# Pooled attention and two feed-forward blocks: the attention scores as two 64-row products in place of one 128-row product with a block-diagonal operand

## The chip, the cores and the metric

The kernel runs on one core of a Trainium2 chip. The metric is the device time of one execution in microseconds (us). Three runs of the kernel before gave a median of 1476.97 us (1474.87 to 1482.33).

## The reference

Attention over keys and values that are averaged eight at a time, then two feed-forward blocks. Batch 8, 8 heads, 576 positions, head size 64, so 72 pooled keys per head:

```
k_p = k.reshape(B, H, Sp, pool, D).mean(axis=3)
v_p = v.reshape(B, H, Sp, pool, D).mean(axis=3)
scores = scale * np.matmul(q, k_p.transpose(0, 1, 3, 2))
scores = scores - np.max(scores, axis=-1, keepdims=True)
attn = np.exp(scores)
attn = attn / (np.sum(attn, axis=-1, keepdims=True) + 1e-09)
out = np.matmul(attn, v_p)
...
a = x @ w1
b = x @ w2
y = ((a * b) @ w3) @ w_out
...
h = y @ w_in
g = h * (1.0 / (1.0 + np.exp(-1.702 * h)))
result = g @ w_out2
```

`x` is the attention output as 4608 tokens of 512 features; w1 and w2 are 512 by 1024, w3 1024 by 1024, w_out 1024 by 512, w_in 512 by 2048, w_out2 2048 by 512.

## The kernel before, in words

Attention works in 32 groups of two heads (`NG`; group n is a batch and a pair of heads). The two heads of a group lie one above the other in the partitions: head 0 in rows 0 to 63, head 1 in rows 64 to 127. For a group,

- `g0` transposes the raw keys and queries on VectorE into `kT` and `qT` (128 rows by 576 positions; one buffer each), adds the keys up eight at a time into `ks` (128 by 72, line 258), and two ScalarE copies (lines 260 and 261) put the upper and the lower half of `ks` onto the diagonal of `kbd`, a 128 by 144 operand whose other two quarters were set to zero once (line 207);
- `g1` multiplies: for each of the five tiles of up to 128 positions (`tt`) one fp32 matmul (line 277) with the 128 by 128 tile of `qT` as the stationary operand and `kbd` as the moving one, so that 144 columns come out, 72 for each head. The first three tiles go to one PSUM bank, the other two to a second one; VectorE takes the maximum of each row and head (line 282) and subtracts it into `s_t` (line 284), bank by bank;
- `g2` is the exponential on ScalarE, `g3` the sum and the division and 32 by 32 transposes on VectorE, `g4` splits the weights into a high and a low part for the product in fp32r, `g6` multiplies by the pooled values (lines 380 to 383) and puts the result into `x`.

For the first four groups (`NPE`), `g4` transposes on TensorE (lines 351 to 361), and odd groups use the banks `acc2` and `acc3` in place of `wk2` and `wk3`.

The first feed-forward block runs in between. Every product of it is made of three fp32r matmuls of 512 columns (`mm3`, lines 114 to 116: high by high, high by low, low by high). `tick()` calls the next step of a group after each half of a feed-forward step, so that four ticks make a group once the first four are through. Weights arrive as 64-bit numbers, are turned into fp32 by `Conv.step` (ScalarE, VectorE, and GpSimd at line 172), and w3 is transposed on TensorE at line 508. A second part of the program (line 709 and on) holds the second feed-forward block and no attention.

The instructions are written by Python in this order, and the tile framework's scheduler sets the final order of each engine; the order within a call of `g1` is therefore not the order on the chip in every group.

An fp32 matmul stands in the trace as two records, each with its own load of the stationary operand (LDWEIGHTS, on the row PEld) and its own MATMUL; an fp32r matmul is one record.

Of the kernel before, what the change touches and what calls it, by code (L numbers as in the profile page):

```python
# [7 lines left out]
F32 = mybir.dt.float32  # L8
# [4 lines left out]
ALU = mybir.AluOpType  # L13
AX = mybir.AxisListType
# [3 lines left out]
P = 128  # L18
# [4 lines left out]
def pooled_attention_moe_moe2(  # L23
# [18 lines left out]
    nc = tc.nc  # L42
    B, H, S, D = q.shape
    NT, DM = out.shape
    POOL = 8
    SK = S // POOL
# [11 lines left out]
    TT = (S + P - 1) // P  # L58
    KW = 2 * SK
# [25 lines left out]
    def take(shape=(P, 2, T), dtype=F32R):  # L85
        pool, i = free.pop(0)
        t = pool.tile(list(shape), dtype, name=f"s{i}", tag=f"s{i}")
        held[id(t)] = (t, pool, i)
        return t

    def take_a(i, dtype=F32R):

        return slota_p.tile([P, 2, T], dtype, name=f"s{i}", tag=f"s{i}")
# [30 lines left out]
    def sl(i, n=P):  # L124
        return slice(i * n, (i + 1) * n)
# [65 lines left out]
    with pa_ctx:  # L191
        pa = pa_ctx.enter_context(tc.tile_pool(name="pa", bufs=1))
# [6 lines left out]
            out=mask[:, 0], in_=mask[:, 0], compare_op=ALU.is_gt, fill=0.0,  # L199
            base=SK, pattern=[[0, D]], channel_multiplier=-1)  # L200
        nc.gpsimd.affine_select(
            out=mask[:, 1], in_=mask[:, 1], compare_op=ALU.is_ge, fill=0.0,
            base=-SK, pattern=[[0, D]], channel_multiplier=1)
        qT = pa.tile([P, TT * P], F32, name="qT")
        nc.vector.memset(qT[:, S:], 0.0)
        kbd = pa.tile([P, 2, SK], F32, name="kbd")
        nc.vector.memset(kbd, 0.0)
        s_sl = take(dtype=F32)
        s_ts = [pa.tile([P, TT, PW], F32, name="s_t"), s_sl.rearrange("p a b -> p (a b)")[
            :, :TT * PW].rearrange("p (t w) -> p t w", w=PW)]  # L210
        for t in s_ts:
# [6 lines left out]
            out=ident, in_=ident, compare_op=ALU.is_equal, fill=0.0,  # L218
# [3 lines left out]
        nc.gpsimd.memset(f32(vt), 0.0)  # L222


        g_q, g_k, g_v, g_s = {}, {}, {}, {}

        def load_blocks(dst, src, b, hp):
            for c in range(4):
# [5 lines left out]
        def g_load(n):  # L234
            if n >= NG:
                return
            b, hp = divmod(n, HP)
            g_k[n] = pa.tile([P, S], F32, name="kr", tag="raw", bufs=4).rearrange("p (g d) -> p g d", d=32)
            load_blocks(g_k[n], k, b, hp)
            g_q[n] = pa.tile([P, S], F32, name="qr", tag="raw", bufs=4).rearrange("p (g d) -> p g d", d=32)  # L240
            load_blocks(g_q[n], q, b, hp)
# [10 lines left out]
        def g0(n):  # L252
            kr, qr = g_k.pop(n), g_q.pop(n)
            kT = pa.tile([P, S], F32, name="kT", tag="kT")
            nc.vector.transpose(out=kT, in_=kr.rearrange("p g d -> p (g d)"))
            nc.vector.transpose(out=qT[:, :S], in_=qr.rearrange("p g d -> p (g d)"))
            ks = pa.tile([P, SK], F32, name="ks", tag="ks")
            nc.vector.tensor_reduce(
                out=ks, in_=kT.rearrange("p (s u) -> p s u", u=POOL), op=ALU.add, axis=AX.X)
            nc.scalar.copy(kbd[:D, 0], ks[:D])  # L260
            nc.scalar.copy(kbd[D:, 1], ks[D:])
            g_load(n + 1)

        def banks_of(n):
            return acc[2:] if n < NPE and n % 2 else wk[2:]

        def s_of(n):
            return s_ts[n % 2 if n < NPE else 0]

        def g1(n):  # L270
            sc, s_t = banks_of(n), s_of(n)
            mov = kbd.rearrange("p a s -> p (a s)")
            nm = pa.tile([P, 2 * TT], F32, name="nm", tag="nm", bufs=2)
            for half, tts in ((0, range(0, 3)), (1, range(3, TT))):
                w = len(tts) * KW
                for i, tt in enumerate(tts):
                    nc.tensor.matmul(  # L277
                        sc[half][:, i * KW:(i + 1) * KW], qT[:, sl(tt)], mov,
                        start=True, stop=True)
                ps = sc[half][:, :w].rearrange("p (a s) -> p a s", s=SK)  # L280
                m = nm[:, 2 * tts[0]:2 * tts[-1] + 2]
                nc.vector.tensor_reduce(out=m, in_=ps, op=ALU.max, axis=AX.X)
                na = 2 * len(tts)
                nc.vector.tensor_tensor(
                    out=s_t[:, tts[0]:tts[-1] + 1, :KW].rearrange("p t (a s) -> p t a s", s=SK),
                    in0=ps.rearrange("p (t a) s -> p t a s", a=2),
                    in1=m.rearrange("p (t a) -> p t a", a=2).unsqueeze(3).to_broadcast(
                        [P, na // 2, 2, SK]),
                    op=ALU.subtract)

        def g2(n):
            s_t = s_of(n)
# [112 lines left out]
        def tick_first():  # L405

            t = tick_n[0]
            tick_n[0] += 1
            for n in range(NPE):
                if t == 2 * n + 6:  # L410
                    g6(n)
            for n in range(NPE):
                s = t - 2 * n
                if s == 0 and n == 0:
                    g0(0)
                elif s == 1:
                    g1(n)
                elif s == 2:
                    g2(n)
                    g0(n + 1)  # L420
                elif s == 3:
                    g3(n)
                elif s == 4:
                    g4(n)
                    g_va(n)
                elif s == 5:
                    g_vb(n)
            if t == 2 * NPE + 4:
                tick_n[0] = 4 * NPE
                give(s_sl)  # L430

        def tick():
            t = tick_n[0]
            if t < 4 * NPE:
                return tick_first()
            tick_n[0] += 1
            n, s = divmod(t, 4)
            if s == 0:
                if NPE <= n - 1 < NG:
                    g4(n - 1)  # L440
            elif s == 1:
                if n < NG:
                    g1(n)
            elif s == 2:
                if NPE <= n - 1 < NG:
                    g6(n - 1)
                if n < NG:
                    g2(n)
                    g_va(n)
                if n + 1 < NG:  # L450
                    g0(n + 1)
            elif n < NG:
                g3(n)
                g_vb(n)
# [147 lines left out]
        for blk in range(NB):  # L602
            x = [x_slot(blk, c) for c in range(KM)]
            if blk == NB - 2:

                pa_ctx.close()
                pa = pa_ctx.enter_context(tc.tile_pool(name="pc", bufs=1, reuse_waits="tile"))
# [10 lines left out]
            for f in range(NF1):  # L618
# [6 lines left out]
                if blk == NB - 1:  # L625
                    give(w1_s.pop(f))
                    give(w2_s.pop(f))
                    if 0 <= f - FA < KM:

                        t = take_a(f - FA)  # L630
# [6 lines left out]
                a = pa.tile([P, T], F32, name="a", tag="a", bufs=2)  # L637
# [34 lines left out]
    with tc.tile_pool(name="pb", bufs=1, reuse_waits="tile") as pb, \  # L672
# [206 lines left out]
        for k, f in enumerate(FO):  # L879
            bk = bank()  # L880
            w = ready.pop(("h", 0, f))
# [29 lines left out]
        for pr in range(1, NPAIR + 1):  # L911
# [17 lines left out]
            for fp in range(NFP):  # L929
# [4 lines left out]
                for name, i in ORDER:  # L934
# [6 lines left out]
                    if name in PART:  # L941
                        s, h = PART[name]
                        w = ready[s, pr, 2 * fp + i][:, h]
                    else:
                        w = ready[name, pr, fp][:, i]
# [66 lines left out]
            m1, U, V, n = [], [], [], 0  # L1012
# [116 lines left out]
```

## Time and profile before

| | |
|---|---|
| median of three runs | 1476.97 us (1474.87 to 1482.33) |
| the profiled execution | 1479.71 us, span 1478.0 us |
| TensorE matmul (PE) busy | 1438.7 us, 97% |
| stationary loads (PEld) busy | 1190.0 us, 81% |
| VectorE (DVE) busy | 988.7 us, 67% |
| ScalarE (ACT) busy | 693.9 us, 47% |
| GpSimd (POOL) busy | 489.0 us, 33% |

Busy shares are means over the whole span. A matmul's record is longer than the time that it adds to a stream, since matmuls overlap; what one adds is read from the distance between the starts of two. PEld lies beside PE. The score matmuls of the 32 groups lie between 24 and 601 us of the span.

### The profile page before, as it was taken

To read this page: it belongs to the slowest core of one execution; us is meant where nothing else is said; L and a number is where in the kernel's file an instruction comes from. 1 tells how busy PE (TensorE), PEld (TensorE's weight loads), DVE (VectorE), ACT (ScalarE), POOL (GpSimd) and SP (SyncE) were. 2 spreads that over 40 slices of the span, in tenths; PEclk is the share of its full clock that TensorE was granted. 3 is DMA by queue.
4 is the path that set the end of the run, shared out by engine and by line. 5 is a ranking of instruction groups with operands and counts; after the bars stand their busy time and mean duration, and the time that the engine had idled before them with its cause. 6 is when DMAs were issued, how large, how long until landed. Compare 5 with 4: busy or idle time off the path is not lost.

```text
span 1478.0 us, 19436 instructions
## 1 busy us (share of the span) xinstructions
PE 1438.7 (97%) x6536; PEld 1190.0 (81%) x6536; DVE 988.7 (67%) x1728; ACT 693.9 (47%) x1212; POOL 489.0 (33%) x589
## 2 busy tenths in 40 slices
PE   6979999999999999999999999999999999999998
PEld 4867888888888888888788887888788888888886
DVE  7888998878787877654737255683559354944554
ACT  7875444434343433366635344552455244534442
POOL 8789656554545555366733100000000000000000
PEclk9989999999999999999999999999999999999999
DMA  9992233323232311199879978877677766785665
GB/s 265 248 233 48 57 85 57 80 46 78 49 77 49 77 33 37 42 325 344 309 236 398 325 243 276 294 211 221 194 244 224 221 197 221 239 234 180 194 213 139
DMA packets 294436, 267.64 MB, mean 181 GB/s; under 512 B 201664, under 2 KB 226240, under 8 KB 294336
## 3 DMA queue, kind: packets, MB, share of 16 engines
q1 hardware_dynamic: 291648, 265.09, 59.8%
q10 hardware_dynamic: 2688, 1.31, 0.3%
q8 instruction: 52, 0.85, 0.2%
q14 instruction: 48, 0.39, 0.1%
HBM read 209.72 MB, written 56.62 MB: 180 GB/s over the span
## 4 chain that ended last, share of the span: by engine, by line
PE 82%; DMA 7%; DVE 5%; ACT 2%; SPq 2%; issue 1%; POOL 1%; DVEq 0%; ACTq 0%; POOLq 0%
PE bk L709 39%; PE wk L114 8%; PE wk L115 8%; PE wk L116 8%; PE acc L114 4%; PE acc L115 4%; PE acc L116 4%; PE wk L277 2%; DMA wud<-wt 2%; DVE p L314 1%; SPq L229 1%; DMA st<-wind 1%; PE bk L115 1%; PE bk L116 1%; PE bk L114 1%
## 5 line engine op out<-in xcount | busy, mean ns | idle before, releaser
L709 PE MATMUL bk<-mv,st 128*128 128x512 f32 x1152 | 272.6, 391 | 0.7 <-DMA st<-wud 0.7
L709 PE MATMUL bk<-xM,st 128*128 128x512 f32 x1092 | 259.0, 390 | 3.9 <-DMA st<-wind 3.7
L709 PEld LDWEIGHTS bk<-mv,st 128*128 128x128 f32 x1152 | 217.3, 189 | 46.3 <-issue 1.1
L709 PEld LDWEIGHTS bk<-xM,st 128*128 128x128 f32 x1092 | 204.5, 188 | 48.6 <-issue 2.5
L114 PE MATMUL wk<-s,s 128*128 128x512 f32 x576 | 227.0, 396 | 2.8 <-DVE a L641 1.2
L116 PE MATMUL wk<-s,s 128*128 128x512 f32 x576 | 224.9, 391 | 2.1 <-DVE s L105 2.1
L115 PE MATMUL wk<-s,s 128*128 128x512 f32 x576 | 224.9, 391 | 0.0
L314 DVE STREAM_TRANSPOSE p<-s_t 32x160 f32<-32x160 f32 (+1 forms) x560 | 178.5, 319 | 10.3
L114 PE MATMUL acc<-s,s 128*128 128x512 f32 x352 | 134.8, 406 | 8.2 <-ACT s L104 3.2
L115 PE MATMUL acc<-s,s 128*128 128x512 f32 x352 | 141.4, 402 | 0.9 <-POOL s L105 0.8
L116 PE MATMUL acc<-s,s 128*128 128x512 f32 x352 | 140.4, 399 | 0.0
L114 PEld LDWEIGHTS wk<-s,s 128*128 128x128 f32 x576 | 108.5, 189 | 26.2 <-DVE a L641 2.1
L116 PEld LDWEIGHTS wk<-s,s 128*128 128x128 f32 x576 | 108.3, 188 | 24.8 <-DVE s L105 2.3
L115 PEld LDWEIGHTS wk<-s,s 128*128 128x128 f32 x576 | 108.4, 188 | 22.1 <-DVE s L391 0.4
L105 DVE TENSOR_TENSOR mv<-g,mv 128x1024 fp32r<-128x1024 f32 x80 | 97.8, 1222 | 33.6 <-ACT mv L104 32.2
L104 ACT CAST mv<-g 128x1024 fp32r<-128x1024 f32 x80 | 84.3, 1054 | 71.8 <-PE bk L709 71.4
L172 POOL TENSOR_TENSOR cv<-cv,s 128x512 int32<-128x512 int32 x72 | 97.5, 1364 | 28.6 <-DVE cv L169 21.1
L105 POOL TENSOR_TENSOR s<-a,s 128x512 fp32r<-128x512 f32 x56 | 72.5, 1294 | 82.5 <-ACT s L104 62.7
L638 ACT COPY a<-wk 128x512 f32<-128x512 f32 x72 | 42.1, 585 | 110.5 <-PE wk L116 89.7
L369 POOL TENSOR_TENSOR ph<-p,ph 128x576 fp32r<-128x576 f32 x32 | 45.7, 1429 | 126.5 <-ACT ph L368 123.9
L114 PEld LDWEIGHTS acc<-s,s 128*128 128x128 f32 x352 | 67.8, 193 | 23.4 <-ACT s L104 5.2
L115 PEld LDWEIGHTS acc<-s,s 128*128 128x128 f32 x352 | 68.2, 194 | 15.0 <-POOL s L105 2.0
(190 smaller groups left out, 2357.9 us busy)
## 6 DMA issues: line engine op xcount, KB each, us to landing
st<-wud SPq DMA_DIRECT2D x96, 512.0 KB, 4.4
st<-wind SPq DMA_DIRECT2D x66, 512.0 KB, 4.7
st<-wind SPq DMA_DIRECT2D x76, 256.0 KB, 3.9
s<-in_moe_w_dram SPq DMA_DIRECT2D x32, 512.0 KB, 6.4
wind<-s SPq DMA_DIRECT2D x32, 512.0 KB, 5.4
s<-in_moe_w_out_dram SPq DMA_DIRECT2D x24, 512.0 KB, 6.5
kr<-in_k_dram SPq DMA_DIRECT2D x128, 72.0 KB, 2.6
qr<-in_q_dram SPq DMA_DIRECT2D x128, 72.0 KB, 2.6
```

The costliest lines, as they stand in the source:

```text
L104: nc.scalar.copy(dst[:, 0], src)
L105: lo_eng.tensor_tensor(out=dst[:, 1], in0=src, in1=f32(dst[:, 0]), op=ALU.subtract)
L114: nc.tensor.matmul(o, a[:, 0, a_sl], b[:, 0, b_sl], start=first, stop=False)
L115: nc.tensor.matmul(o, a[:, 0, a_sl], b[:, 1, b_sl], start=False, stop=False)
L116: nc.tensor.matmul(o, a[:, 1, a_sl], b[:, 0, b_sl], start=False, stop=last)
L172: nc.gpsimd.tensor_tensor(out=w.bitcast(I32), in0=w.bitcast(I32), in1=lo_w.bitcast(I32), op=ALU.add)
L229: nc.sync.dma_start(dst[32 * c:32 * c + 32], src[b, 2 * hp + c // 2, :, 32 * (c % 2):32 * (c % 2) + 32].rearrange("(g t) d -> t g d", t=32))
L277: nc.tensor.matmul(sc[half][:, i * KW:(i + 1) * KW], qT[:, sl(tt)], mov, start=True, stop=True)
L314: nc.vector.transpose(out=dst[:, :nt, 32 * c:32 * c + 32], in_=s_t[32 * c:32 * c + 32, :nt, 32 * r:32 * r + 32])
L369: nc.gpsimd.tensor_tensor(out=ph[:, 1], in0=s0, in1=f32(ph[:, 0]), op=ALU.subtract)
L638: nc.scalar.copy(a, pa_)
L709: nc.tensor.matmul(o, w[:, x, m], b[:, y], start=first and n == 0, stop=last and n == 2, skip_group_check=True)
```

## The change

Each head has a product of its own. For every tile of positions there are two fp32 matmuls, one on rows 0 to 63 and one on rows 64 to 127 of the array (`tile_position` (0, 0) and (64, 0)): the stationary operand is 64 rows by 128 columns of `qT`, the moving one 64 rows by 72 columns of `ks`. Head 0 goes to the first bank, head 1 to the second, five tiles of 72 columns in each. Maximum and subtraction go by head instead of by half of the tiles. `kbd`, its memset and its two copies are gone; `ks` itself is read by TensorE.

```diff
-        kbd = pa.tile([P, 2, SK], F32, name="kbd")
-        nc.vector.memset(kbd, 0.0)
...
-            nc.scalar.copy(kbd[:D, 0], ks[:D])
-            nc.scalar.copy(kbd[D:, 1], ks[D:])
+            g_ks[n] = ks
...
         def g1(n):
-            sc, s_t = banks_of(n), s_of(n)
-            mov = kbd.rearrange("p a s -> p (a s)")
-            nm = pa.tile([P, 2 * TT], F32, name="nm", tag="nm", bufs=2)
-            for half, tts in ((0, range(0, 3)), (1, range(3, TT))):
-                w = len(tts) * KW
-                for i, tt in enumerate(tts):
+            sc, s_t, ks = banks_of(n), s_of(n), g_ks.pop(n)
+            nm = pa.tile([P, 2, TT], F32, name="nm", tag="nm", bufs=2)
+            for tt in range(TT):
+                for h in range(2):
+                    hd = slice(h * D, (h + 1) * D)
                     nc.tensor.matmul(
-                        sc[half][:, i * KW:(i + 1) * KW], qT[:, sl(tt)], mov,
-                        start=True, stop=True)
-                ps = sc[half][:, :w].rearrange("p (a s) -> p a s", s=SK)
-                m = nm[:, 2 * tts[0]:2 * tts[-1] + 2]
-                nc.vector.tensor_reduce(out=m, in_=ps, op=ALU.max, axis=AX.X)
-                na = 2 * len(tts)
+                        sc[h][:, tt * SK:(tt + 1) * SK], qT[hd, sl(tt)], ks[hd],
+                        start=True, stop=True, tile_position=(h * D, 0))
+            for h in range(2):
+                ps = sc[h][:, :TT * SK].rearrange("p (t s) -> p t s", s=SK)
+                nc.vector.tensor_reduce(out=nm[:, h], in_=ps, op=ALU.max, axis=AX.X)
                 nc.vector.tensor_tensor(
-                    out=s_t[:, tts[0]:tts[-1] + 1, :KW].rearrange("p t (a s) -> p t a s", s=SK),
-                    in0=ps.rearrange("p (t a) s -> p t a s", a=2),
-                    in1=m.rearrange("p (t a) -> p t a", a=2).unsqueeze(3).to_broadcast(
-                        [P, na // 2, 2, SK]),
-                    op=ALU.subtract)
+                    out=s_t[:, :, h * SK:(h + 1) * SK], in0=ps,
+                    in1=nm[:, h].unsqueeze(2).to_broadcast([P, TT, SK]), op=ALU.subtract)
```

The built order of TensorE around one burst of scores in the later groups, before (line 277; `wk_72` and `wk_73` are the two score banks, `wk_70` and the `acc` tiles belong to the feed-forward block):

```order
L115 MATMUL acc_69<-s_3472,s_690 128x512
L116 MATMUL acc_69<-s_3472,s_690 128x512
L277 MATMUL wk_72<-kbd,qT 128x144 x3
L277 MATMUL wk_73<-kbd,qT 128x144 x2
L114 MATMUL wk_70<-s_2083,s_1375 128x512
```

and the same place now (line 273 is the score matmul of the changed kernel):

```order
L115 MATMUL acc_69<-s_3336,s_1129 128x512
L116 MATMUL acc_69<-s_3336,s_1129 128x512
L273 MATMUL wk_72<-ks,qT 128x72
L273 MATMUL wk_73<-ks,qT 128x72
L273 MATMUL wk_72<-ks,qT 128x72
L273 MATMUL wk_73<-ks,qT 128x72
```

The five matmuls have become ten, which change between the two heads; six more rows like the last two follow before the next line 114. The last 20 groups and the first four have this order.

The same engine in one of the groups between these (groups 4 to 11), before:

```order
L114 MATMUL acc_67<-s_1406,s_808 128x512
L277 MATMUL wk_73<-kbd,qT 128x144 x2
L115 MATMUL acc_67<-s_1406,s_808 128x512
L116 MATMUL acc_67<-s_1406,s_808 128x512
L277 MATMUL wk_72<-kbd,qT 128x144 x3
L114 MATMUL acc_68<-s_1406,s_808 128x512
```

and now:

```order
L116 MATMUL wk_70<-s_711,s_1471 128x512
L273 MATMUL wk_73<-ks,qT 128x72 x3
L273 MATMUL wk_72<-ks,qT 128x72 x4
L273 MATMUL wk_73<-ks,qT 128x72
L273 MATMUL wk_72<-ks,qT 128x72
L273 MATMUL wk_73<-ks,qT 128x72
L114 MATMUL wk_70<-s_823,s_1471 128x512
```

Here the scheduler has put several matmuls of one head behind one another; in all there are 36 unbroken bursts now, where there were 41.

## Rows read from the trace of the kernel before

**Rows 1.** TensorE by windows: window, length, PE busy (records), granted clock, DMA share, GB/s.

```profile
0.00:100.00 100.00, 78.79 (x361) 0.93 0.97 250
100.00:200.00 100.00, 94.83 (x445) 0.98 0.40 84
200.00:610.00 410.00, 410.00 (x1981) 1.00 0.26 56
```

**Rows 2.** Chain of waits in order of time, 430 to 460 us: start, length, what.

```profile
431.70 1.23 PE wk L277 x10
...
450.37 1.23 PE wk L277 x10
```

**Rows 3.** Groups by line on TensorE, 200 to 610 us: line, shapes, count, busy, mean.

```profile
L277 PE MATMUL wk<-kbd,qT 128*128 128x144 f32 x220 | 31.0, 285 | 0.0
```

**Rows 4.** Timeline of PE near 308 us: start, length, engine, line, operation, tiles, shapes.

```profile
308.19 0.29 PE L380 MATMUL wk<-ph,vm 128*128 128x288 f32 x1
308.32 0.30 PE L381 MATMUL wk<-ph,vm 128*128 128x288 f32 x1
```

**Rows 5.** Timeline of PEld, 23.9 to 24.06 us.

```profile
23.96 0.19 PEld L277 LDWEIGHTS wk<-kbd,qT 128*128 128x128 f32 x1 [1.18 <-ACT kbd L261]
```

**Rows 6.** Timeline of PEld, 24.15 to 24.18 us: the second load of that burst.

```profile
24.07 0.19 PEld L277 LDWEIGHTS wk<-kbd,qT 128*128 128x128 f32 x1
```

**Rows 7.** Timeline of PE, 60.9 to 62.6 us.

```profile
61.71 0.27 PE L508 MATMUL wk<-ident,cv 128*128 128x128 f32 x1
61.82 0.27 PE L360 MATMUL acc<-ident,s 128*32 128x128 f32 x1
62.02 0.23 PE L361 MATMUL acc<-ident,s 64*32 64x64 f32 x1
```

**Rows 8.** Timeline of PE, 38.0 to 39.3 us.

```profile
38.48 0.23 PE L361 MATMUL wk<-ident,s_t 64*32 64x64 f32 x1
38.64 0.50 PE L115 MATMUL acc<-s,s 128*128 128x512 f32 x1
38.98 0.40 PE L116 MATMUL acc<-s,s 128*128 128x512 f32 x1
39.22 0.39 PE L115 MATMUL acc<-s,s 128*128 128x512 f32 x1
```

**Rows 9.** Timeline of PEld, 62.1 to 62.22 us: loads of 32 and of 128 columns.

```profile
62.02 0.09 PEld L361 LDWEIGHTS acc<-ident,s 64*32 64x32 f32 x1 [0.21 <-issue]
62.18 0.14 PEld L508 LDWEIGHTS wk<-ident,cv 128*128 128x128 f32 x1
```

**Rows 10.** Timeline of PEld, 62.325 to 62.34 us: the load after that.

```profile
62.24 0.14 PEld L508 LDWEIGHTS wk<-ident,cv 128*128 128x128 f32 x1
```

**Rows 11.** Timeline of PEld, 56.9 to 57.9 us: a load of 64 rows.

```profile
57.36 0.14 PEld L354 LDWEIGHTS acc<-ident,s 64*128 64x128 f32 x1 [0.17 <-issue]
```

**Rows 12.** Groups by line and shape, whole run: shapes, count, busy, mean, idle before.

```profile
L277 PEld LDWEIGHTS wk<-kbd,qT 128*128 128x128 f32 x300 | 42.2, 191 | 4.5 <-ACT kbd L261 1.2 <-DVE s L391 0.2
...
L282 DVE TENSOR_REDUCE nm<-wk 128x6 f32<-128x432 f32 x30 | 17.8, 595 | 1.3 <-PE wk L277 1.3
...
L284 DVE TENSOR_TENSOR s_t<-wk,nm 128x432 f32<-128x432 f32 x30 | 17.3, 578 | 0.0
...
L284 DVE TENSOR_TENSOR s_t<-wk,nm 128x288 f32<-128x288 f32 x30 | 13.2, 440 | 0.0
L282 DVE TENSOR_REDUCE nm<-wk 128x4 f32<-128x288 f32 x30 | 13.2, 440 | 0.0
...
L260 ACT COPY kbd<-ks 64x72 f32<-64x72 f32 x32 | 8.0, 249 | 3.7 <-DVE ks L258 3.5
L261 ACT COPY kbd<-ks 64x72 f32<-64x72 f32 x32 | 8.0, 249 | 0.7
```

More of the change, by code (lines that the diff above doesn't have):

```diff
@@ L222, in pooled_attention_moe_moe2 @@
         nc.gpsimd.memset(f32(vt), 0.0)
-        g_q, g_k, g_v, g_s = {}, {}, {}, {}
+        g_q, g_k, g_v, g_s, g_ks = {}, {}, {}, {}, {}
         def load_blocks(dst, src, b, hp):
```

## The prediction

> **What bounds the kernel.** I read the busy time by windows first. From 200 to 610 us TensorE is busy without a gap, at the full granted clock, 2.4 GHz; before that it is not: it has 21.2 us of idle time in the first 100 us and 5.2 us in the next 100 [rows 1]. So there are two stretches with different rules. In the later one whatever TensorE gains or loses is gained or lost by the kernel; in the earlier one part of it falls into waits for ScalarE, VectorE and GpSimd.
>
> Then the chain of waits: every 18.67 us (450.37 less 431.70) it goes for 1.23 us through the ten records of the score matmuls of one group [rows 2]. So a score burst costs 1.23 us, of a record 0.123 us, and 32 bursts cost 39.4 us. 220 of the records lie from 200 us on [rows 3]: 22 groups in the full stretch, ten before it. After 601 us there are no scores, and the second block keeps its code.
>
> Then single records, to see what makes up 0.123 us. A record has to load its stationary operand and to stream its moving columns. A matmul of 288 columns is followed by the next after 0.13 us [rows 4]; a score record with 144 columns takes 0.123 us, so an fp32 record streams each column about twice. With 72 columns that is 0.06 us, estimated by proportion. The load: at the start of the first burst, where nothing streams, the second load begins 0.11 us after the first [rows 5, 6]. Today the load of the next record (0.11) hides behind the stream of this one (0.12). Both are nearly equal; **halving the stream leaves the load bare**.
>
> **The change part by part.**
>
> *Records.* Five fp32 matmuls become ten, so ten records become twenty, each with a load of 128 columns and a stream of 72. What a load of 64 rows costs in fp32 no row shows. From below: the loads of the fp32 transposes (another kind of matmul) take 0.06 us where one is bare, 62.24 less 62.18 [rows 9, 10]. From above: 0.11 [rows 5, 6]. Whether half of the rows makes a load shorter can be read from the lengths of such transposes' loads: 0.14 us with 128 rows and 128 columns [rows 9], 0.14 with 64 rows and 128 columns [rows 11], 0.09 with 64 rows and 32 columns [rows 9]. Length goes with columns, and the columns stay 128. So I take 0.11, the row of the same operation. If loads follow one another, a burst has 20 x 0.11 = 2.20 us of loads, and the last stream of 0.06 behind them.
>
> The Trainium skill, "TensorE: Matmul & The Clock Gate", section on LDWEIGHTS, speaks against this change in the same way: the time of a load goes by its columns, and 32 rows take as long as 128. By its formula (128 columns at 1.2 GHz) I estimate 107 ns, and the twenty loads would be 2.13 us in place of 2.20; the trace agrees as far as its rows reach.
>
> *Changing the shape of the array.* The changed bursts go from 128 rows to 64 and back. The program has four places with a 64-row matmul. Between two 128-row transposes 0.11 us pass (61.71 to 61.82), before a 64-row one 0.20 (to 62.02) [rows 7]: 0.09 more on the way in. On the way out, the 64-row matmul (64 columns, 0.05 us at the rate of the 0.11 for 128) is followed after 0.16 us [rows 8]: another 0.11. And the next matmul cannot hide its load: 0.34 to the one behind it instead of 0.24 [rows 8], 0.10 to 0.11. Together 0.31 us a burst. From below, nothing, if what these rows show belongs to the change of the column width there (32 columns) and not of the rows; I take 0.31, since entering L360 with 32 columns shows no such step (0.11).
>
> *Sum of a burst:* 2.20 + 0.06 + 0.31 = 2.57 us, 1.34 more than 1.23. In the full stretch: 22 x 1.34 = +29.5 us. Of the ten groups before 200 us I count half, between all and nothing, since TensorE partly waits there anyway: 10 x 1.34 / 2 = +6.7 us.
>
> *What goes away.* Two copies of 0.249 us a group on ScalarE [rows 12]. From 200 us on, TensorE never waits for it, so they are worth nothing there. In the first groups they stand between the sum of the keys and the first load: the whole run has 1.2 us of waits of the loads for line 261 [rows 12]. I take -0.7 us; the bounds are 0 and -2. The memset of `kbd` is one early VectorE instruction: nothing.
>
> *VectorE.* Two maxima and two subtractions a group before and after: (595 + 440) and (578 + 440) ns for 6 + 4 head-tiles [rows 12] become twice five, the same sum by proportion. Both banks are now complete only at the end of the burst, instead of the first one after three fifths of it; the one wait known there is 1.3 us in the whole run [rows 12]. Nothing, while TensorE has other work; at most another 1 us early. `ks` has one buffer and is now read by the matmuls, so the sum of the next group (line 258) waits for them; `qT`, also with one buffer, is refilled on the same engine after the same matmuls already, so no new wait arises. GpSimd's instructions and the DMA issues stay the same in number; where the scheduler sets them otherwise in the first groups, I count nothing. The four bursts more than groups (36 against 32) would cost 4 x 0.31 = 1.2 us, inside the half that is open there.
>
> *Sum:* 29.5 + 6.7 - 0.7 = +35.5 us on the profiled execution's 1479.71 us, which is 2.7 us above the median of the runs: 1515.2 there, **1512 us** against the median.
>
> **Rivals.**
>
> *1. The loads of the two halves run side by side.* In the last 20 groups, and the first four, the matmuls change between the heads, so the load for rows 64 to 127 could lie beside that for rows 0 to 63. No row shows two loads at once, nor one that forbids it. Two records then cost one load: 10 x 0.11 + 0.06 + 0.31 = 1.47 us, +0.24 a burst. In groups 4 to 11 one head's matmuls stand behind one another and stay at +1.34. Sum: 20 x 0.24 + 2 x 1.34 + 6 x 1.34 / 2 + 4 x 0.24 / 2 - 0.7 = +11.3, so 1488 us. The Trainium skill, "TensorEngine Tiling (Array Packing)", section Tiling Modes, says just this, that different tiles may load and multiply in parallel, and also that a change of mode drains the array; the second half agrees with the 0.31 us above, the first half no run here shows yet.
>
> *2. Faster: the halves cost no more than their streams.* If loads also shrink to less than the stream, a pair costs 0.06 us, ten pairs 0.60. It decides for the change when a pair of records costs under 0.092 us ((1.23 - 0.31) / 10); with 0.06 a burst saves 0.32, over 20 groups -6.4. In groups 4 to 11 there are no pairs: 20 x 0.06 + 0.31 is 0.34 more than now, +0.7 for the last two of them and +1.0 for six at half, and the first four give -0.6: about -6 with the copies, 1471 us. If the change of shape is free too, a pair saves all of its half: -0.63 x 20 - 1.3 - 0.7, about -14.6, 1462 us. Against it speaks that loads follow their columns.
>
> *3. Loads that no longer hide at all* in 64-row form: 20 x (0.11 + 0.06) + 0.31 = 3.71 us, +2.48 a burst, 54.6 + 12.4 - 0.7 = +66, 1543 us. Against it: in 128-row form the load hides behind the stream of the same rows.
>
> *4. Nothing that can be measured:* loads side by side and the change of shape free make 1.16 us a burst, close to today's: about 1477 us.
>
> **How the numbers follow.** Forecast (loads one after another) 0.46, rival 1 0.27, rival 2 0.13, rival 3 0.07, rival 4 0.07. The forecast's own range: 1505 if the early groups cost nothing (29.5 - 0.7), 1520 if they cost all of 1.34 (42.9). Rival 1 reaches from 1481 (early groups free, 0.2 for the shape) to 1494 (early groups whole). The range also takes in rival 4, 3 us to either side: 1474 to 1521. It leaves out rivals 2 and 3, 0.20 together. Half a per cent, 7.4 us, is about what a measurement of this kernel can tell from no change. Slower by more: the forecast, rival 3 and four fifths of rival 1: 0.75. Within: rival 4, the rest of rival 1 and a little of rival 2: 0.14. Faster by more: most of rival 2: 0.11.
>
> **What would show it.** In the changed profile the distance between the starts of two score records should be near 0.11 us in the full stretch, with the chain through a burst at 2.4 to 2.6 us in place of 1.23, and the distance between bursts near 20 us in place of 18.67. If pairs start together or every 0.11 us, rival 1 holds. A first feed-forward matmul behind a burst that starts its successor after 0.34 rather than 0.24 shows the bare load. TensorE's busy share between 200 and 640 us should stay whole. The forecast is wrong if a burst lasts under 1.5 us, or if the time goes to waits before 200 us, from the scheduler's other order there.

## The result: 1498.47 us, 1.4% slower, and the profile after

Four runs of the changed kernel gave a median of 1498.47 us (1497.20 to 1499.52), four of the kernel before on the same chip 1477.02 us (1474.87 to 1482.33). The ratio is 1.014, with a 95% interval of 1.0126 to 1.0155: slower by 21.5 us. The profiled execution has a span of 1495.5 us, 17.5 us more than the one of the kernel before; the sums below are made against these 17.5 us.

TensorE by windows, after (columns as in [rows 1], then the other engines):

```profile
0.00:100.00 100.00, 79.96 (x402) 59.16 (x403) 72.48 (x118) 76.50 (x152) 78.11 (x94) 0.92 0.90 249
100.00:200.00 100.00, 92.05 (x449) 74.67 (x448) 84.44 (x177) 45.67 (x96) 74.29 (x98) 0.96 0.32 71
200.00:620.00 420.00, 419.05 (x2215) 347.17 (x2214) 335.79 (x822) 154.14 (x321) 214.32 (x306) 1.00 0.26 57
```

The full stretch is still full: 419.05 of 420 us at the full granted clock. Between 100 and 200 us TensorE now idles 8.0 us in place of 5.2 [rows 1].

The chain of waits, after, 400 to 460 us, the rows that answer to [rows 2]:

```profile
410.19 1.27 PE wk L273 x20
...
429.13 1.27 PE wk L273 x20
```

Twenty records take hardly longer on the chain than ten did, and the bursts come every 18.94 us in place of 18.67. What a burst adds in all is seen in the timeline of PE around one, after and (second fence) before:

```profile
580.21 0.39 PE L116 MATMUL acc<-s,s 128*128 128x512 f32 x1
580.52 1.34 PE L273 MATMUL wk<-ks,qT 64*128 64x72 f32 x20
581.79 0.50 PE L114 MATMUL wk<-s,s 128*128 128x512 f32 x1
582.13 0.39 PE L115 MATMUL wk<-s,s 128*128 128x512 f32 x1
```

```profile
580.73 0.39 PE L116 MATMUL acc<-s,s 128*128 128x512 f32 x1
580.95 1.39 PE L277 MATMUL wk<-kbd,qT 128*128 128x144 f32 x10
582.08 0.49 PE L114 MATMUL wk<-s,s 128*128 128x512 f32 x1
582.41 0.40 PE L115 MATMUL wk<-s,s 128*128 128x512 f32 x1
```

From the start of the last feed-forward matmul ahead of the burst to the start of the second one behind it, 1.92 us pass now (580.21 to 582.13) and 1.68 passed before (580.73 to 582.41). Without a burst the same two steps take 0.454 us, so a burst costs 1.467 us now and 1.234 before, by the records' unrounded starts. All 20 bursts from 258 us on cost 1.467 or 1.468. In their single records the two heads start 0.007 us apart, and such pairs follow every 0.112 us: ten pairs, each in the time of one load.

Where the scheduler put matmuls of one head behind one another it is otherwise. Timeline of PE, after, in one of the groups 4 to 11:

```profile
219.64 0.39 PE L114 MATMUL wk<-s,s 128*128 128x512 f32 x1
219.96 1.33 PE L273 MATMUL wk<-ks,qT 64*128 64x72 f32 x10
221.22 0.50 PE L115 MATMUL wk<-s,s 128*128 128x512 f32 x1
...
222.11 1.33 PE L273 MATMUL wk<-ks,qT 64*128 64x72 f32 x10
223.37 0.50 PE L115 MATMUL wk<-s,s 128*128 128x512 f32 x1
```

Ten records of one head take as long as twenty that alternate, and this group has two such bursts: 2.93 us. The five other bursts between 150 and 240 us cost 1.745 (three times), 1.970 and 2.192 us.

Most of the rest is one wait. The waits of PE, after (line waited for; us in all, times, longest):

```profile
PE wk L500 <- POOL cv L172: 10.2, 2, 8.7
PE wk L114 <- DVE a L633: 7.4, 2, 6.4
```

The first was there before (10.4 us, line 508 of the kernel before); the second was 1.2 us. The timelines of VectorE, of GpSimd and of TensorE around it, all after:

```profile
115.70 0.82 DVE L105 TENSOR_TENSOR s<-cv,s 128x512 fp32r<-128x512 f32 x1
...
118.73 6.83 DVE L105 TENSOR_TENSOR s<-cv,s 128x512 fp32r<-128x512 f32 x1
125.48 6.64 DVE L306 STREAM_TRANSPOSE p<-s_t 32x160 f32<-32x160 f32 x20
132.16 1.09 DVE L169 TENSOR_SCALAR cv<-cv 128x512 uint32<-128x512 uint32 x1
133.17 0.68 DVE L633 TENSOR_TENSOR a<-wk,a 128x512 f32<-128x512 f32 x1
```

```profile
118.18 1.29 POOL L105 TENSOR_TENSOR s<-cv,s 128x512 fp32r<-128x512 f32 x1
119.44 0.72 POOL L316 TENSOR_TENSOR va<-vr 128x256 f32<-128x256 f32 x1
...
123.73 1.28 POOL L105 TENSOR_TENSOR s<-cv,s 128x512 fp32r<-128x512 f32 x1
126.53 0.32 POOL L334 TENSOR_TENSOR vt<-vtf,vt 32x64 fp32r<-32x64 f32 x1 [1.52 <-issue]
```

```profile
127.11 0.39 PE L116 MATMUL acc<-s,s 128*128 128x512 f32 x1
133.91 0.80 PE L114 MATMUL wk<-s,s 128*128 128x512 f32 x1 [6.41 <-DVE a L633]
```

Read them together. One VectorE instruction, a split of a weight tile with two operands, took 6.83 us where one of the same shape took 0.82 three microseconds earlier. GpSimd had no pause from 112.7 to 125.0. Seven of its instructions, from 118.18 on, lie beside the long one, which ended half a microsecond after the last of them. Twenty transposes stand behind it on VectorE and then the addition of line 633, for whose result TensorE idles 6.41 us.

An unbroken row of GpSimd is not all that it takes: the instruction of 0.82 us (115.70) ran inside that same row. The kernel before has a milder case:

```profile
139.76 3.33 DVE L105 TENSOR_TENSOR s<-cv,s 128x512 fp32r<-128x512 f32 x1
```

It stood behind three GpSimd instructions and ended at 143.1, while GpSimd worked on without a pause to beyond 144; no wait of TensorE hangs on it. What decides how long such an instruction stands is not shown.

The wait also leaves TensorE at a lower clock. Timeline of PE behind it, and the window 134 to 138 us (columns as in [rows 1], then the other engines):

```profile
134.50 0.63 PE L115 MATMUL wk<-s,s 128*128 128x512 f32 x1
134.00:138.00 4.00, 4.00 (x10) 3.17 (x11) 4.00 (x7) 1.98 (x4) 3.85 (x5) 0.50 0.19 33
```

The granted clock is 0.50 there, the 1.2 GHz level, after 6.41 us without a matmul, and is back at 2.4 GHz from 138.8 us on. The eleven matmuls from 133.91 to 138.76 take 4.85 us; at 0.34 us for the first step and 0.227 for each of the others, as elsewhere at the full clock, they would take 2.6. So the lower clock costs about 2.2 us more.

So the 17.5 us of the profile come to: 20 x 0.233 = 4.7 for the alternating bursts; 4.9 for the six groups between 150 and 240 us (12.33 us in all, less 6 x 1.236); 6.2 for the wait on line 633 (7.4 less 1.2); and 1.7 that remain for everything else in the first 240 us and the second block. The 2.2 us of lower clock behind the wait are in these 1.7, and all else together takes 0.5 of them back.

### The profile page after: what moved, and what is told of

It is laid out like the page before. It is cut to its first block, busy times and chain, and to the rows that moved or that the text cites. A ratio compares the mean times of both kernels' runs of the same rounds, so it can differ in the third digit from the quotient of the medians.

```text
span 1495.5 us, 20011 instructions
## 1 busy us (share of the span) xinstructions
PE 1453.8 (97%) x6856; PEld 1191.1 (80%) x6856; DVE 986.9 (66%) x1727; ACT 682.4 (46%) x1148; POOL 486.7 (33%) x589
## 4 chain that ended last, share of the span: by engine, by line
PE 84%; DMA 6%; DVE 5%; SPq 1%; ACT 1%; issue 1%; POOL 1%; DVEq 0%; ACTq 0%; POOLq 0%
PE bk L701 39%; PE wk L114 9%; PE wk L115 8%; PE wk L116 8%; PE acc L115 4%; PE acc L116 4%; PE acc L114 4%; PE wk L273 2%; DMA s<-in_moe_w_dram 2%; DMA wud<-wt 2%; PE bk L114 1%; PE bk L115 1%; PE bk L116 1%; SPq L227 1%; DVE s L105 1%
## 5 line engine op out<-in xcount | busy, mean ns | idle before, releaser
L306 DVE STREAM_TRANSPOSE p<-s_t 32x160 f32<-32x160 f32 (+1 forms) x560 | 178.5, 319 | 10.9 <-DVE s_t L295 0.5
```

The source lines that it names most:

```text
L306: nc.vector.transpose(out=dst[:, :nt, 32 * c:32 * c + 32], in_=s_t[32 * c:32 * c + 32, :nt, 32 * r:32 * r + 32])
```

## The experiments

Which part costs what is hard to read from one trace, since a wait early in the program can take in a loss or make one. The following table is used below: the start of the n-th feed-forward matmul (lines 114 to 116, n counted from 0) in each profile, less its start in the kernel before, in us. A constant row means that nothing more is lost; "end" is the difference of the spans.

| n | 250 | 300 | 600 | 1000 | 2780 | end |
|---|---|---|---|---|---|---|
| kernel before, at | 122.0 | 135.5 | 216.9 | 321.6 | 764.0 | 1478.0 |
| the change | 2.1 | 10.1 | 13.2 | 15.1 | 18.9 | 17.5 |
| heads in turn, order kept | 3.5 | 2.6 | 3.5 | 5.1 | 8.9 | 4.0 |
| change in the last 20 groups | 2.3 | 1.4 | 1.5 | 2.8 | 6.6 | 2.3 |
| change in the first 12 groups | 5.1 | 10.9 | 13.9 | 14.4 | 14.4 | 9.9 |
| one split on GpSimd | 1.1 | 1.1 | 6.5 | 8.4 | 12.3 | 11.6 |
| quarters | 2.0 | 3.6 | 5.3 | 6.4 | 3.1 | 5.9 |
| quarters, last 20 groups | 3.0 | 2.0 | 2.0 | 0.7 | -3.3 | -0.1 |
| quarters from group 6 | 0.4 | -0.5 | 0.2 | 0.2 | -3.7 | -6.5 |

After the 2780th matmul no kernel differs from the one before in its code, yet the last column moves by -4.9 to +3.2 us against the one ahead of it. That is the uncertainty of such a sum.

### The heads in turn everywhere

The changed kernel, with each score matmul held behind the one written before it, so that the scheduler can't put one head's together:

```diff
-                    nc.tensor.matmul(
-                        sc[h][:, tt * SK:(tt + 1) * SK], qT[hd, sl(tt)], ks[hd],
-                        start=True, stop=True, tile_position=(h * D, 0))
+                    with tc.issue_after(last) if last is not None else ExitStack():
+                        mm = nc.tensor.matmul(
+                            sc[h][:, tt * SK:(tt + 1) * SK], qT[hd, sl(tt)], ks[hd],
+                            start=True, stop=True, tile_position=(h * D, 0))
+                    last = mm.ins
```

> The ten matmuls of every group keep the written order, head 0 and head 1 in turn (an issue-order edge from each to the one before it); nothing else differs from the changed kernel. Theory S (a pair of different heads shares the time of one load; neighbours of one head pay two, so the mixed bursts of groups 4 to 11 are what the early stretch lost): every burst in one piece at 1.47 us, 32 x 0.23 = +7.5 us on before at most, 1481 to 1488 us. Rival W (the early stretch lost its time to waits and to another order of the scheduler, not to the bursts' length): within 3 us of the changed kernel's 1498.5.

Measured: 1485.26 us against 1477.62 for the kernel before there, ratio 1.0055 (1.0035 to 1.0074). Every burst from group 5 on costs 1.467 or 1.468 us, and the long VectorE instruction is gone (the longest of its kind takes 2.17 us). Timeline of PE around a burst:

```profile
589.13 0.39 PE L116 MATMUL acc<-s,s 128*128 128x512 f32 x1
589.45 1.34 PE L275 MATMUL wk<-ks,qT 64*128 64x72 f32 x20
590.72 0.50 PE L114 MATMUL wk<-s,s 128*128 128x512 f32 x1
```

Of the 21.5 us of the change, 13.9 hang on the order within the bursts and on what that order does to the other engines; 7.6 stay when all bursts alternate, where 32 x 0.233 makes 7.5. Such a close match is in part luck: the table has 8.9 us at n = 2780 and 4.0 at the end.

### One head after the other everywhere

The kernel of the last experiment (kept order), with the loop over the heads outside:

```diff
-            for tt in range(TT):
-                for h in range(2):
+            last = None
+            for h in range(2):
+                for tt in range(TT):
```

> All five matmuls of head 0 are issued ahead of the five of head 1, in every group; the same work as the changed kernel. Theory S (loads run side by side only between different halves of the rows): a burst of the full stretch goes from 1.47 to about 2.4 to 2.57 us, 20 x 1.0 = +20 us on the changed kernel, 1514 to 1524 us. Rival Q (a 64-row record costs half of a 128-row one whatever stands beside it): bursts stay at 1.47, 1495 to 1500 us.

Measured: 1510.08 us, ratio 1.0223 (1.0193 to 1.0254). Timeline of PE:

```profile
453.04 0.39 PE L116 MATMUL acc<-s,s 128*128 128x512 f32 x1
453.36 2.06 PE L275 MATMUL wk<-ks,qT 64*128 64x72 f32 x20
455.35 0.50 PE L114 MATMUL wk<-s,s 128*128 128x512 f32 x1
455.69 0.39 PE L115 MATMUL wk<-s,s 128*128 128x512 f32 x1
```

This is the order in which the forecast's sum should hold, and even here it doesn't hold whole: a burst costs 2.192 us, not 2.57. Records of one head do follow one another every 0.112 us, but a second row of ten, also 0.112 us apart, begins at 454.09, when the first is at its seventh record, so that four pairs lie beside each other. Matmuls on the other half of the rows start before those in front of them in the queue.

### The change in some of the groups alone

The changed code for the last 20 groups and the old code for the first 12, and the reverse:

```diff
+        def g1(n):
+            (g1_half if n >= 12 else g1_full)(n)
```

> Groups 0 to 11 as before the change, groups 12 to 31 as in the changed kernel. If a burst in turn costs 0.23 to 0.26 us more than the one of before, whatever stands ahead: 20 x 0.25 = +5 us, 1480 to 1484 us. Rival (the length of the program and its order as a whole make the loss): 1490 or more.

> Groups 0 to 11 as in the changed kernel, groups 12 to 31 as before the change. If the loss of the first stretch is the mixed bursts and what they bring with them: the rest of the 21.5 us, +13 to +18, 1490 to 1495 us. Rival (the loss comes with the bursts of the full stretch): 1480 or less.

Measured: 1481.51 us, ratio 1.0021 (1.0010 to 1.0031), with the last groups changed; 1487.33 us, ratio 1.0061 (1.0040 to 1.0082), with the first (1481.97 to 1489.79 in five runs). So the last 20 bursts cost 3.9 us, where their lengths alone make 4.9 (the first of them is mixed, 1.745 us, the others alternate). In the first 12 groups the same long instruction comes back, and with it the wait (timelines of VectorE and of TensorE):

```profile
120.38 6.83 DVE L105 TENSOR_TENSOR s<-cv,s 128x512 fp32r<-128x512 f32 x1
```

```profile
135.56 0.80 PE L114 MATMUL wk<-s,s 128*128 128x512 f32 x1 [5.05 <-DVE a L663]
```

The table has the whole loss of this kernel before n = 700, none behind it. The two parts make 13.6 us together (3.9 and 9.7), the whole change 21.5. In the profiles it is 2.3 + 9.9 = 12.2 against 17.5. There they do add up to n = 2780, 6.6 + 14.4 = 21.0 against 18.9; behind it, where nothing is changed, the three profiles get 4.3, 4.5 and 1.4 us back. So what is missing in the sum of the profiles lies in the second block. That the medians miss their 7.9 us for the same reason is not shown.

### Twice the loads at the same streams

The changed kernel with each product in two of 36 columns: the streams stay in sum, the loads double.

```diff
+                for kk in range(2):
+                    for h in range(2):
+                        hd = slice(h * D, (h + 1) * D)
+                        c = tt * SK + kk * HK
+                        nc.tensor.matmul(
+                            sc[h][:, c:c + HK], qT[hd, sl(tt)], ks[hd, kk * HK:(kk + 1) * HK],
+                            start=True, stop=True, tile_position=(h * D, 0))
```

> Each product of 72 columns is made as two of 36 columns with the same stationary operand; the scheduler keeps the two heads in turn in the full stretch. The columns streamed stay the same in total, the loads double. Theory S (0.112 us a pair is the time of the loads): 20 pairs x 0.112 + 0.35 = 2.59 us a burst in place of 1.47, +22 to +28 us on the changed kernel, 1520 to 1528 us. Rival T (0.112 us is two streams of 0.056, one behind the other): bursts stay near 1.47 us, 1495 to 1503 us.

Measured: 1536.47 us, ratio 1.0401 (1.0378 to 1.0424). The chain of waits, 400 to 460 us:

```profile
415.55 2.35 PE wk L276 x40
435.57 2.35 PE wk L276 x40
```

Half the columns, and the pairs still follow every 0.112 us: 20 of them, and a burst of 2.554 us, 1.09 more than with ten pairs. The load sets the distance, not the stream. By the reading of the table above, this kernel is 58.0 us behind at n = 2780: 27.8 of them come after n = 600, as 21 bursts of 1.32 more than before want, and 16.6 were lost by n = 60 already, in the first 62 us. That loss was not expected, and it puts the time above the 1520 to 1528 us that were. Part of it is the clock: between 20 and 60 us the granted clock is 0.74, 0.75, 0.83 and 0.77 in each ten us, where the kernel before has 1.00, 0.66, 1.00 and 1.00. The rest stays open.

### One 64-row matmul alone

The kernel before, with one 64-row matmul behind the ten records of each group. Its 72 columns go to the free end of the second bank and are read by nobody.

```diff
+                if half:
+                    nc.tensor.matmul(
+                        sc[1][:, w:w + SK], qT[:D, sl(0)], kbd[:D, 0],
+                        start=True, stop=True, tile_position=(0, 0))
```

> The kernel of before with one more fp32 matmul in each burst, on 64 rows with 72 columns, behind the five; its output is read by nobody. Theory S (the change of shape costs 0.31 us a burst, two bare loads 0.22 and the last stream 0.06 come on top): about +0.55 to +0.6 us a burst, 20 to 32 times, 1488 to 1495 us. Rival (the change of shape is free): two loads behind the streams, +0.15 to +0.22 a burst, 1480 to 1484 us.

Measured: 1498.00 us, ratio 1.0140 (1.0120 to 1.0161). Timeline of PE:

```profile
465.25 0.39 PE L116 MATMUL acc<-s,s 128*128 128x512 f32 x1
465.48 1.39 PE L277 MATMUL wk<-kbd,qT 128*128 128x144 f32 x10
466.79 0.44 PE L281 MATMUL wk<-kbd,qT 64*128 64x72 f32 x2
467.16 0.50 PE L114 MATMUL wk<-s,s 128*128 128x512 f32 x1
467.50 0.40 PE L115 MATMUL wk<-s,s 128*128 128x512 f32 x1
```

A single 64-row matmul makes a burst 0.565 us longer, 1.799 in place of 1.234. Of that 0.11 is its second load. The last 128-row record starts at 466.58; 0.21 us pass to the first 64-row load and 0.20 from the second 64-row record (466.96) to line 114. The kernel with this one matmul is as slow as the changed one, though it keeps everything else: entering and leaving the 64-row form is a price of its own. Of the 20.6 us, 22 x 0.565 = 12.4 lie in the full stretch (by the table's reading, 8.1 us are lost at n = 600 and 20.9 at 2780). The time is above the 1488 to 1495 us expected: 32 x 0.565 is 18.1, and the other 2.5 us are not accounted for.

### Quarters: four places, loads of 64 columns

The changed kernel with 64 positions a matmul in place of 128, at four places of the array (two halves of the rows, two halves of the columns), in kept order:

```diff
+                for c in range(2):
+                    for h in range(2):
...
+                            mm = nc.tensor.matmul(
+                                sc[h][c * D:(c + 1) * D, tt * SK:(tt + 1) * SK],
+                                qT[hd, sl(2 * tt + c, D)], ks[hd],
+                                start=True, stop=True, tile_position=(h * D, c * D))
```

> Every product is cut once more, by positions: four matmuls of 64 rows by 64 columns at four places of the array for each tile of 128 positions (20 a group, in the written order), each with a load of 64 columns and a stream of 72. Theory S (a load takes its columns' time, and loads at different places of the array run side by side): 0.06 us for a set of four records in place of 0.112 for two, 10 x 0.06 + 0.35 = 0.95 to 1.0 us a burst against 1.23 before, 1468 to 1473 us, faster than before. Rival U (places side by side in the columns share their load path, or a record has a least time of 0.11 us): 20 x 0.112 + 0.35 = 2.6 us, 1515 us or more. Between them (loads of 64 columns, but one after another within the same rows): 20 x 0.06 + 0.35 = 1.55 us, 1484 to 1488 us.

Measured: 1483.02 us, ratio 1.0043 (1.0028 to 1.0059). Chain of waits, 400 to 460 us:

```profile
400.12 0.79 PE wk L276 x40
418.59 0.79 PE wk L276 x40
```

The burst does what it should: 0.985 us, a quarter less than before, with four records in 0.0625 us. The table shows 32 such gains overtaken: up to n = 600 it has lost 5.3 us, from there to n = 2780 it wins 2.2, where its 21 bursts alone would win 5.2, and the second block loses 2.8. The waits of PE in the first 240 us have, in place of 1.2 us before, 5.0 for line 638, the same addition:

```profile
PE wk L114 <- DVE a L638: 5.0, 4, 2.9
```

A smaller burst is thus not enough; the expectation counted the bursts and not the first stretch.

### One split of a weight tile on the other engine

The changed kernel with the one VectorE instruction that took 6.83 us put on GpSimd (the fifth tile of w2):

```diff
-            conv.add(col_tile(w2, f), None, conv.to(w2_s, f, nc.vector))
+            conv.add(col_tile(w2, f), None, conv.to(w2_s, f, nc.gpsimd if f == 4 else nc.vector))
```

> The changed kernel with one instruction given to another engine: the low part of the fifth tile of w2, the VectorE subtraction that stood for 6.83 us at 118.7 us in the changed kernel's trace beside an unbroken row of GpSimd instructions, is made by GpSimd; VectorE's order ahead of it and the bursts stay. Theory M (some 6 us of the loss are that one encounter, into which the new order of the first stretch ran by chance): TensorE's wait of 6.4 us for line 633 goes, 1490 to 1494 us. Rival (TensorE is late there for another reason, which shows at the next wait): 1496 to 1500 us.

Measured: 1492.19 us against 1478.71 for the kernel before there, ratio 1.0091 (1.0069 to 1.0114): 13.5 us slower than before where the change is 21.5 slower. Timelines of VectorE and of GpSimd at the place:

```profile
117.87 6.66 DVE L306 STREAM_TRANSPOSE p<-s_t 32x160 f32<-32x160 f32 x20
124.56 0.69 DVE L633 TENSOR_TENSOR a<-wk,a 128x512 f32<-128x512 f32 x1
```

```profile
117.21 1.29 POOL L105 TENSOR_TENSOR s<-cv,s 128x512 fp32r<-128x512 f32 x1
...
124.01 1.27 POOL L105 TENSOR_TENSOR s<-cv,s 128x512 fp32r<-128x512 f32 x1
```

GpSimd has its unbroken run as before, with one instruction more; VectorE now does its transposes beside it, in 6.66 us, against 6.64 in the changed kernel, where GpSimd stood still for most of them, and line 633 comes 8.6 us sooner (1.0 of them it was ahead already). TensorE's long gap is gone; up to n = 300 this kernel has lost 1.1 us in place of 10.1. At n = 600 it is 6.5 in place of 13.2: of the 9.0 us saved, 2.3 are lost again, where a wait of 1.8 us for line 633 stands in place of one of 0.9. So the long wait is that one instruction's. That GpSimd blocked it is read from the two timelines; a kernel that thins out GpSimd's work at that place and leaves VectorE's alone was not tried.

### Quarters in the later groups

The kernel before, with quarters for the last 20 groups and for the last 26:

```diff
+        def g1(n):
+            (g1_half if n >= 12 else g1_full)(n)
```

```diff
+        def g1(n):
+            (g1_half if n >= 6 else g1_full)(n)
```

> Groups 0 to 11 as before the change, groups 12 to 31 in quarters (64 rows by 64 columns), whose burst takes 0.985 us against 1.234. Theory (each burst of the full stretch goes straight into the time): 20 x 0.25 = 5 us less, 1471 to 1474 us beside 1477.4 for before, faster than both kernels by little. Rival (what TensorE gains there waits for DMA at the start of the second block): 1476 to 1479 us.

> The same from group 6 on, so 26 groups in quarters: 26 x 0.25 = 6.5 us less than before if the order of the stretch from 140 to 260 us brings no new encounter, 1469 to 1473 us; if it does, as in the kernel with all groups in quarters, 1476 us or more.

Measured: 1476.19 us, ratio 0.9969 (0.9952 to 0.9986), and 1476.33 us, ratio 0.9979 (0.9966 to 0.9992), both against 1478.71. Both are faster than the kernel before, by 0.2 to 0.3%, and by less than the 5.0 and 6.5 us of their bursts (0.25 each). In the profile of the first the bursts' gain is there up to n = 2780 (from +2.0 to -3.3), and the second block, whose code is the same, gives 3.2 us of it back. TensorE, 860 to 960 us, there and (second fence) in the kernel before:

```profile
860.00:960.00 100.00, 94.28 (x398) 76.46 (x397) 60.20 (x81) 49.01 (x68) 0.00 (x0) 0.97 0.83 273
```

```profile
860.00:960.00 100.00, 96.68 (x417) 78.70 (x416) 61.92 (x83) 51.25 (x71) 0.00 (x0) 0.98 0.86 286
```

The waits there are mostly for the DMAs that bring the weights of the second block. In the profile of the second kernel that block gains 2.8 us instead; the first profile is 3.5 us above the median of its kernel, the second 3.2 below. Whether an earlier start of that block as such runs into its transfers, or the difference is from run to run, these runs don't tell.

## Why the prediction was right in its sign and wrong in its main step

- **That the full stretch passes on what a burst costs** held: it is full after the change too, and the table's rows grow there by the burst's price (15.1 to 18.9 for the change between n = 1000 and 2780, with 16 bursts of 0.233).
- **The load is left bare, and costs 0.11 us whatever its rows** held: pairs every 0.112 us, the same with half the columns to stream, and 0.0625 us where the load has 64 columns. These rows agree with what the prediction takes from the Trainium skill, "TensorE: Matmul & The Clock Gate", section LDWEIGHTS (loading the stationary operand): the time of a load goes by its columns.
- **0.31 us for the change of shape** held within some hundredths: ten pairs of 0.112 us leave 0.35 of the 1.467 for the change and the last stream, for which the sum had 0.31 + 0.06. The added matmul shows 0.21 us on the way in and 0.20 on the way out, with a bare load of 0.11 behind each.
- **The failed step** is the one ahead of the sum: "If loads follow one another, a burst has 20 x 0.11 = 2.20 us of loads". Taken as the likeliest, at 0.46, it gave 2.57 us a burst. The prediction's own sign of being wrong, a burst under 1.5 us, came true. The last 20 groups cost 1.467, the figure of rival 1, which stood at 0.27. Where the order is by head, at least, loads do follow one another, and even there 2.192 was measured, as four pairs overlap across the heads. The row behind the step was of 128-row loads only; no row had two loads in different halves, and the choice between the rivals stood on none.
- **Rival 1's own sum, 1488 us,** was 11.3 us over the kernel before; 21.5 were measured. Its bursts were about right: 0.24 more for an alternating one was taken and 0.233 measured. For the groups between, 1.34 more was taken, 1.70 measured in the worst and 0.51 to 0.96 in the five mixed ones. What it lacks is the next point.
- **"Where the scheduler sets them otherwise in the first groups, I count nothing"** failed: in the new order one VectorE instruction fell beside GpSimd's unbroken run, and the wait behind it costs 6 to 8 us (6.2 by the waits, to which the lower clock adds 2.2; 8.0 by the run with the split moved).
- **Half of ten early bursts** can't be checked by itself: with heads in turn everywhere, 2.6 us are lost by n = 300, before which TensorE also waits elsewhere.
- **The copies** were put at -0.7 us. The first score burst starts at 23.84 us in place of 23.99; beyond these 0.15 us no run tells a gain from them.

The forecast of 1512 us was too high by 13.5 because its bursts were too dear by 20 x 1.1 = 22 us, while 6 to 8 us that it didn't count came on top of what was left. The measured time lies between the two sums that the prediction worked out, 1505 to 1520 for the forecast and 1481 to 1494 for rival 1. It is inside the stated 1474 to 1521 because that range covers the gap as well, and because two errors worked against each other. That part is luck. (In rival 2, 20 x 0.06 + 0.31 is 0.28 more than 1.23 and not 0.34; that moves the rival by 0.3 us.)

## What to carry to other kernels

Before an fp32 matmul is cut into row tiles, compare its stream with its load: where the moving operand has 72 columns, two half-height loads side by side take what one whole load takes, so halving the stream saves nothing and the change of form (about 0.3 us a visit here) is paid on top. Cutting the stationary operand's columns is what shortened the load here (64 columns: 0.0625 us a set of four), though of this kernel it took only 0.2 to 0.3%, and only where the first groups stayed as they were. And tiles in different rows should take turns in the final order, not only in the source. Where TensorE also waits for other engines, as in the first 240 us here, a new order can cost about as much as the change itself (6 to 8 us beside 7.6), so look at the timeline of the first stretch before trusting a sum of bursts.

## What the runs showed of the hardware that was not expected

- Two loads in different halves of the rows lie beside each other: starts 0.007 us apart, 0.112 us a pair; four in quarters, 0.0625 us a set. The Trainium skill, "TensorEngine Tiling (Array Packing)", section Tiling Modes, says that different tiles may load and multiply in parallel; these runs agree.
- The matmuls of the other half don't wait for all in front of them: written head by head, the second head's first record starts with the first head's seventh.
- Going from 128-row to 64-row matmuls and back costs about 0.3 us (0.35 with the last stream, whose 0.06 is the prediction's estimate), and one 64-row matmul between 128-row ones 0.565 us.
- A VectorE instruction with two operands in SBUF can take 6.83 us in place of 0.82 beside an unbroken row of GpSimd instructions, while one-operand transposes beside such a row go at their own speed (20 in 6.66 us). That GpSimd is the cause is read from the timelines and not tested. The Trainium skill, "SBUF — State Buffer", section SBUF: two separate sides, says that of such a VectorE instruction and a GpSimd one that reads SBUF, whichever starts first holds the shared ports for the whole instruction and the other is blocked. The timelines fit this, with seven GpSimd instructions going by first.
- After 6.41 us without a matmul TensorE ran at the 1.2 GHz level (granted clock 0.50) from 133.9 to 138.8 us, which added about 2.2 us to that wait.
